# Seven half-width products in place of two full ones: a Strassen step over token halves in the first layer of one token group

## The chip, the cores and the metric

One core of a Trainium2 chip runs the kernel. The metric is device time in microseconds (us) of one launch; the kernel before takes 520.27 us, the median of 3 runs (520.02 to 520.69). The engines are named as in the profile: PE is TensorE (matmuls), PEld its weight loads, DVE is VectorE, ACT is ScalarE, POOL is GpSimd, SP is the engine on whose queue nearly all DMA transfers are issued.

## The reference

A linear attention with decay makes x, and two multilayer products follow. Everything is float32.

```
attn_out = _attn_ref(q, k, v, lam)         # 2 batches, 8 heads, 768 positions, 64 wide
x = attn_out.transpose(0, 2, 1, 3).reshape(1536, 512)

h = x @ w_in                               # 512 x 2048
x = maximum(0.01 * h, h) @ w_out           # 2048 x 512

a, b = x @ w1, x @ w2                      # 512 x 1024 each
out = ((a * b) @ w3) @ w_out2              # 1024 x 1024, 1024 x 512
```

## The kernel before

The 1536 tokens are worked on in three groups of 512, g = 0, 1, 2. The hidden width of 2048 is cut into 16 slices of 128, f = 0 to 15. A float32 operand is held as two halves in the type that TensorE takes, a high part and the rest, and one product of float32 matrices is three matmuls per piece (`EXACT`: high x high, low x high, high x low). Tokens are the moving side, so h comes out transposed, 128 hidden units by 512 tokens, in one PSUM bank.

For one slice and one group the first layer is `unit_h` (line 757 on): 4 chunks of the model width x 3 = 12 matmuls of 128x512 by `full` (line 731) into a PSUM buffer `ps`. ACT then applies the leaky step in place and copies the high part out, VectorE subtracts to get the low part (`pair_ops`, line 740). The second layer is `unit_y` (line 806): 12 matmuls of 128x512 by `products` (line 738) into four accumulators `acc`.

In the first 90 us the attention chunks are made, with slices 0 to 3 between them. The other slices come in blocks of four, b = 4, 8, 12. In such a block the groups 1 and 2 are taken together: `unit_hpair` (matmuls on line 1434) does the first layer for a pair of slices by Strassen's seven products over two slices and two groups, and `unit_joint` (line 1604) the second layer. It uses three PSUM buffers, one for each chain of sums. Group 0 is done slice by slice with `unit_h` and `unit_y`. `h_sums` makes the sums and differences of w_in that the seven products need (tile `sx`). Then `unit_w` (line 1297), the product of w_out with w1 and w2, `unit_pair` (line 1013) and `unit_out` (line 1200) follow.

The order of the instructions of each engine is written out by a list planner, `in_order` (line 81): each operation has a rank, a cost in ns (`CHIP`, `MB` for transfers), what it comes after, and the buffers that it takes and uses; an operation is put on its engine's list when the planner's clock says that its inputs and buffers are there, in the order of rank. Each engine then runs its list in order, and semaphores hold an instruction until its inputs are there. Transfers of weights go through a ring of `raw` buffers and are converted on ACT, VectorE and POOL (`top`, `u`, `f`: lines 328, 334, 352). Lines 224 and 228 are the helpers that write the high part and the low part of a pair.

Of the kernel before, what the change touches and what calls it, by code (L numbers as in the profile page):

```python
# [7 lines left out]
F32 = mybir.dt.float32  # L8
F32R = mybir.dt.float32r
# [5 lines left out]
ALU = mybir.AluOpType  # L15
# [17 lines left out]
EXACT = ((0, 0), (1, 0), (0, 1))  # L33
XB = (10,40,45,50,50,60,85,105)
XL = (10,40,125,50,50,60,145,165)
# [7 lines left out]
class Buf:  # L43
# [6 lines left out]
    def free(self, now):  # L50
        return all(u.end is not None and u.end <= now for u in self.users)


class Op:
# [5 lines left out]

    def __init__(self, cost, fn, rank, after=(), takes=(), uses=(), behind=(), port=False, lag=None, hold=0):
# [3 lines left out]
        self.lag, self.hold = lag, hold  # L65
        for b in (*takes, *uses):
            b.users.append(self)


EARLY = [32, 103, 104]  # L70
LATENCY = {"q": 3600}
MB = 2560
CHIP = {
    ("act", 680): 662, ("act", 580): 520, ("act", 560): 490, ("act", 500): 490, ("act", 350): 305, ("dve", 640): 602,
    ("dve", 680): 602, ("dve", 660): 602, ("dve", 400): 335, ("dve", 1180): 1135, ("pool", 1250): 1255,
    ("pool", 640): 700,
}
SEEN = {"dve": 115, "act": 130, "pool": 80, "pe": 100}

# [76 lines left out]
def tile_kernel(ctx: ExitStack, tc, qkv, lamb, w_in, w_out, w1, w2, w3t, wo, out):  # L156
# [32 lines left out]
    }  # L189
    pools.update({r: const for r in TAGS})  # L190
    ops = []

# [104 lines left out]
    def convert(kind, i, rank):  # L297
# [42 lines left out]
        def whole(e):  # L340
# [20 lines left out]
        o0 = op(  # L361
            {"q": MB / 2}, load, EARLY[len(loads) - 1] if len(loads) <= len(EARLY) else rank, takes=[raw], behind=late
        )
# [376 lines left out]
    def pair_ops(src_op, ps, rank):  # L740
# [12 lines left out]
        return buf, [o1, o2]  # L753

    gp, accs, acc_op, last_h = {}, {}, {}, []

# [19 lines left out]
    def accumulate(tag, g, f, nf, rank, w_ops, bufs, job, pairs, evac):  # L776
# [14 lines left out]

        if first and g == NG - 1:
            for c in range(4):
                after.append(op({"pe": 680}, mm([c], False), rank, after, [acc[c]], bufs, behind=after[-1:]))
            acc_op[tag, g] = after[-1]
            return
        if f % nf < nf - 1:
# [581 lines left out]
    hm_home = {}  # L1379
    sums = {}  # L1380

    def h_sums(f, rank):
# [11 lines left out]
        out = []  # L1394
        for get, after, fb in ((g0, [o2, o4], b0), (g1, [o1, o3], b1)):
# [8 lines left out]
        sums[f] = out  # L1404

# [107 lines left out]
    def unit_joint(b, rank, ranks):  # L1513
# [31 lines left out]
        def half(name, which, rank, after=lambda u: []):  # L1545
            out = []
            for u in two:
                d, o = hidden[u]
                buf = Buf("lp" if last else "part")
                parts.append(buf)  # L1550
# [4 lines left out]
                ops_ = halves_of(  # L1555
                    part, lambda t=d[which]: t.tile, [o[which], *opened], [buf], [d[which]], rank,
                    lambda buf=buf: new(buf, [P, 2, T], F32R), ("dve",) if last else ("dve", "pool"),
                )
                out.append((part, ops_, buf))
# [10 lines left out]

        last, parts = b == NF1 - FB, []
        opened = last_op if last else []
        r = ranks["make"]
# [61 lines left out]

    joint_pe, last_op = [], []

# [87 lines left out]
    for k, (g, f) in enumerate(steps[:-2]):  # L1725
        unit_y(g, f, r(k))
        for n, d in CHUNKS.get(k, {}).items():
            attention(n, r(k) + d, n % CPG > 0)
            if n % CPG == CPG - 1:
                outputs(n, r(k) + d + 2)  # L1730
        if steps[k + 2] == (0, FB):
            x_differences(r(k) + 20)
        unit_h(*steps[k + 2], r(k) + 10, r(k + 2))
    PP = (0, 10, 30, 35, 50, 60, 70)
    h_sums(FB, r(len(steps)))
    rank = r(len(steps) - 2)
    for b in range(FB, NF1, FB):
        last = b + FB == NF1
        if b in PAIRED:
            XO = XL if last else XB  # L1740
            unit_y(0, b, rank)
            unit_hpair(b, rank + XO[0])
            unit_h(0, b + 2, rank + XO[1], rank + XO[1] + 20)
            unit_y(0, b + 1, rank + XO[2])
            unit_h(0, b + 3, rank + XO[3], rank + XO[3] + 20)
            if last:
                last_part.append(Buf("xy"))
                last_op.append(
                    op({"dve": 50}, lambda e: new(last_part[0], [P, 2, NCC, T], F32R), rank, [last_h[-1]], [last_part[0]])
                )  # L1750
# [16 lines left out]
        if b in PAIRED:  # L1767
            unit_joint(b, rank + 120, {"sums": rank + 100, "make": rank + 100, "p": [rank + 120 + k for k in ((0, 10, 20, 30, 40, 50, 60) if last else PP)]})
            if not last:
                unit_h(0, b + FB, rank + 140, rank + 230)  # L1770
                unit_h(0, b + FB + 1, rank + 160, rank + 240)
                h_sums(b + FB, rank + 210)
        else:
# [97 lines left out]
```

## Time and profile before

| | |
|---|---|
| median of 3 runs | 520.27 us |
| the profiled execution | 520.21 us |
| its span, first to last instruction | 518.3 us |
| PE busy | 510.6 us, 99% of the span |
| PEld / DVE / ACT / POOL busy | 422.9 / 385.7 / 328.8 / 142.4 us |
| moved by DMA | 54.03 MB, 104 GB/s in the mean |

Busy times are sums over the span, so an engine that is busy 74% of the span in the mean can still be busy all the time in one stretch. A run of instructions in the chain of waits has a start, a length and a count; length by count is the distance from one to the next. The mean length of one matmul as shown elsewhere is longer than that distance, since matmuls overlap.

### The profile page before, as it was taken

To read this page: it belongs to the slowest core of one execution; us is meant where nothing else is said; L and a number is where in the kernel's file an instruction comes from. 1 tells how busy PE (TensorE), PEld (TensorE's weight loads), DVE (VectorE), ACT (ScalarE), POOL (GpSimd) and SP (SyncE) were. 2 spreads that over 40 slices of the span, in tenths; PEclk is the share of its full clock that TensorE was granted. 3 is DMA by queue.
4 is the path that set the end of the run, shared out by engine and by line. 5 is a ranking of instruction groups with operands and counts; after the bars stand their busy time and mean duration, and the time that the engine had idled before them with its cause. 6 is when DMAs were issued, how large, how long until landed. Compare 5 with 4: busy or idle time off the path is not lost.

```text
span 518.3 us, 8618 instructions
## 1 busy us (share of the span) xinstructions
PE 510.6 (99%) x3320; PEld 422.9 (82%) x3320; DVE 385.7 (74%) x640; ACT 328.8 (63%) x627; POOL 142.4 (27%) x128
## 2 busy tenths in 40 slices
PE   8999999999999999999999899999999999999997
PEld 7788887888888888888888688888888888888886
DVE  6876475997588964889799999888347865656951
ACT  5895765776757667457876796886347444454820
POOL 4331021401152411832222223010112635553200
PEclk9999999999999999999999999999999999999999
DMA  8983750222210501017240474870001000000102
GB/s 310 410 339 118 250 205 3 83 81 82 69 56 17 185 2 40 1 56 269 99 145 1 164 242 138 290 261 2 0 1 59 22 1 0 1 1 2 40 21 101
DMA packets 16024, 54.03 MB, mean 104 GB/s; under 512 B 1904, under 2 KB 2416, under 8 KB 15984
## 3 DMA queue, kind: packets, MB, share of 16 engines
q1 hardware_dynamic: 15552, 53.22, 29.2%
q8 instruction: 26, 0.43, 0.4%
q10 hardware_dynamic: 432, 0.27, 0.2%
q14 instruction: 14, 0.11, 0.1%
HBM read 50.34 MB, written 3.15 MB: 103 GB/s over the span
## 4 chain that ended last, share of the span: by engine, by line
PE 87%; DVE 6%; DMA 4%; ACT 1%; issue 1%; SPq 0%; DVEq 0%
PE ps L731 21%; PE acc L738 15%; PE ps L1013 15%; PE ps L1434 10%; PE ps L1297 7%; PE acc L1604 7%; PE acc L1200 5%; PE ps L640 3%; PE ps L1200 2%; DMA raw<-in_w_in_dram 2%; DVE xy L228 2%; DVE yf L1620 2%; DMA yf<-in_qkv_dram 1%; PE ps L720 1%; DVE dd L869 1%
## 5 line engine op out<-in xcount | busy, mean ns | idle before, releaser
L328 ACT CAST top<-raw 128x512 f16<-128x512 bf16 x72 | 56.0, 783 | 18.3 <-DVE few_f L352 7.5
L738 PE MATMUL acc<-act,wp 128*128 128x512 f32 x252 | 61.5, 392 | 0.0
L738 PEld LDWEIGHTS acc<-act,wp 128*128 128x128 f32 x252 | 46.9, 188 | 9.9
L731 PE MATMUL ps<-xy,wp 128*128 128x512 f32 x192 | 44.8, 389 | 0.0
L731 PEld LDWEIGHTS ps<-xy,wp 128*128 128x128 f32 x192 | 36.0, 188 | 7.5
L731 PE MATMUL ps<-xy,wi 128*128 128x512 f32 x168 | 40.9, 393 | 0.9 <-ACT xy L556 0.8
L731 PEld LDWEIGHTS ps<-xy,wi 128*128 128x128 f32 x168 | 31.1, 188 | 8.5 <-ACT xy L556 1.2
L1297 PE MATMUL ps<-wi,wp 128*128 128x512 f32 x144 | 34.7, 392 | 1.4 <-POOL wp L228 0.7
L1013 PE MATMUL ps<-xy,wp 128*128 128x512 f32 x144 | 34.2, 391 | 0.0
L1013 PE MATMUL ps<-xy,raw 128*128 128x512 f32 x144 | 33.9, 389 | 0.0
L334 ACT ACTIVATE u<-raw 128x512 uint32<-128x512 uint32 x50 | 33.4, 669 | 0.0
L1297 PEld LDWEIGHTS ps<-wi,wp 128*128 128x128 f32 x144 | 26.9, 188 | 7.9 <-POOL wp L228 1.2
L228 DVE TENSOR_TENSOR act<-ps,act 128x512 fp32r<-128x512 f32 x32 | 21.9, 684 | 13.7 <-ACT act L746 13.5
L1013 PEld LDWEIGHTS ps<-xy,wp 128*128 128x128 f32 x144 | 26.9, 188 | 6.1 <-DVE w L1031 0.4
L1013 PEld LDWEIGHTS ps<-xy,raw 128*128 128x128 f32 x144 | 27.0, 188 | 5.6
L1620 DVE TENSOR_TENSOR yf<-acc,yf 128x512 f32<-128x512 f32 x28 | 18.8, 684 | 7.1 <-PE acc L1604 7.1
L731 PE MATMUL ps<-xy,few_wi 128*128 128x512 f32 x96 | 23.1, 389 | 0.0
L738 PE MATMUL acc<-wp,act 128*128 128x512 f32 x96 | 22.9, 389 | 0.0
L767 ACT ACTIVATE ps<-ps 128x512 f32<-128x512 f32 x24 | 14.1, 588 | 11.2 <-PE ps L731 11.0
L738 PEld LDWEIGHTS acc<-wp,act 128*128 128x128 f32 x96 | 18.0, 188 | 3.7
L731 PEld LDWEIGHTS ps<-xy,few_wi 128*128 128x128 f32 x96 | 18.0, 188 | 3.7
L352 DVE SCALAR_TENSOR_TENSOR f<-u,top 128x512 uint32<-128x512 uint32 x26 | 18.2, 704 | 3.7 <-ACT u L334 3.6
(318 smaller groups left out, 1254.7 us busy)
## 6 DMA issues: line engine op xcount, KB each, us to landing
raw<-in_w_in_dram SPq DMA_DIRECT2D x16, 512.0 KB, 4.3
raw<-in_w_out_dram SPq DMA_DIRECT2D x16, 512.0 KB, 4.0
raw<-in_w3t_dram SPq DMA_DIRECT2D x16, 512.0 KB, 4.3
raw<-in_w_dram SPq DMA_DIRECT2D x16, 512.0 KB, 5.1
yf<-in_qkv_dram SPq DMA_DIRECT2D x14, 512.0 KB, 7.0
inp<-in_qkv_dram SPq DMA_DIRECT2D x10, 512.0 KB, 9.1
raw<-in_wo_dram SPq DMA_DIRECT2D x8, 512.0 KB, 4.5
out_dram<-f SPq DMA_DIRECT2D x10, 256.0 KB, 2.0
```

Of the source, the lines that this page charges most:

```text
L228: engines[e].tensor_tensor(out=dst(), in0=src(), in1=hi_().bitcast(F32), op=ALU.subtract)
L328: nc.scalar.copy(dst, src)
L334: nc.scalar.activation(out=t, in_=mid, func=AF.Copy, bias=4096.0)
L352: nc.vector.scalar_tensor_tensor(out=get().bitcast(U32), in0=u.tile, scalar=13, in1=top.tile, op0=ALU.logical_shift_right, op1=ALU.bitwise_or,
L731: nc.tensor.matmul(o, w(a)[:, cc * P : (cc + 1) * P], x(b, cc), start=k == 0, stop=k == 3 * NCC - 1)
L738: nc.tensor.matmul(o, st(a), mv(b), start=first and k == 0, stop=last and k == 2)
L1013: nc.tensor.matmul(ps.tile, w(a, kk), mv(b, kk), start=fresh and kk == 0 and i == 0, stop=kk == NCC // 2 - 1 and i == 2, skip_group_check= ...
L1200: nc.tensor.matmul(o, wl(v, t, c), mv(v2)[:, cut], start=begun and t == 0 and i == 0, stop=t == n - 1 and i == 2, skip_group_check=True,)
L1297: nc.tensor.matmul(ps.tile, w(a)[:, k * P : (k + 1) * P], wo_part[j](b), start=j == 0 and n == 0, stop=j == NF2 - 1 and n == 2,)
L1434: nc.tensor.matmul(ps.tile, w(a, kk), mv(b, kk), start=fresh and kk == 0 and i == 0, stop=kk == NCC // 2 - 1 and i == 2, skip_group_check= ...
L1604: nc.tensor.matmul(ps.tile, st[left][k][0](a, c), mv[right][k][0](b_), start=fresh and k == 0 and i == 0, stop=k == 1 and i == 2, skip_gro ...
L1620: nc.vector.tensor_tensor(out=y(), in0=ps.tile, in1=y(), op=ALU.add)
```

## The change

For the pairs of slices (6,7), (8,9), (10,11), (12,13) and (14,15) group 0's `unit_h` is replaced by `unit_hself`. It takes two slices and the two halves of the group's 512 tokens, and makes seven products over half of the model width: 2 chunks x 3 = 6 matmuls of 128x256 each, 42 for a pair in place of 24 of 128x512. Two PSUM buffers of 128x512, `one` and `two`, hold the results, and their halves are token halves. Three copies on ACT (line 1506) and three adds on VectorE (line 1513), all 128x256, combine the products.

The moving side of the products is seven forms of x: three of its corners (b11, b21, b22) and four sums (t1 to t4), each split in a high and a low part. `x_forms` makes them once, at step 6 of the attention phase, and stores them in DRAM (line 1412, 14 transfers); each pair loads its seven forms again (line 1480, 512 KB each, 35 loads) into four slots of a buffer that was opened for the last block only, and is now opened earlier. Beside that the second layer of group 0 is put later by a rank of 43, and for two of four slices it is written as four pieces of three matmuls; the ranks of one product, two costs of the planner and the order of `h_sums` change.

```diff
-XB = (10,40,45,50,50,60,85,105)
+XB = (10,40,45,50,15,60,85,105)
...
+PIECES = (0, 1)
+YB0 = 43
+SELF = (165, 170, 230)
...
-MB = 2560
+MB = 2660
...
+    def x_forms(rank):
...
+            def store(e):
+                t = forms[name] = dram.tile([P, 2, T], F32, tag=f"form_{name}", name=f"form_{name}")
+                for v in range(2):
+                    nc.sync.dma_start(out=t[:, v, :].rearrange("p (k n) -> p k n", n=h), in_=src(v))
...
+    def unit_hself(f, rank, rank_next, order=(0, 0, 0, 0, 0, 0, 0), ahead=30):
...
+        one, two = Buf("ps"), Buf("ps")
+        one_left, one_right, two_left = (one, slice(0, h)), (one, slice(h, T)), (two, slice(0, h))
...
+            def load(e):
+                t = new(mv, None)
+                nc.sync.dma_start(out=t.bitcast(F32), in_=forms[right])
...
+                for kk in range(NCC // 2):
+                    for i, (a, b) in enumerate(EXACT):
+                        nc.tensor.matmul(
+                            ps.tile[:, cut], w(a, kk), mv.tile[:, b, kk * h : (kk + 1) * h],
...
+                {"act": 350}, lambda e: nc.scalar.copy(new(buf, [P, T])[:, :h], ps.tile[:, cut]), rank_next, [o], [buf], [ps]
...
+                lambda e: nc.vector.tensor_tensor(
+                    out=ps.tile[:, dst], in0=ps.tile[:, cut], in1=t.tile[:, :h], op=ALU.add
...
+        p1 = product(0, one_right, "a11", "b11", [])
+        t1, k1 = keep(one_right, p1)
+        p7 = product(1, two_left, "s3", "t3", [])
+        p2 = product(2, one_left, "a12", "b21", [p1])
+        p6 = product(3, one_right, "s2", "t2", [k1])
+        t2, k2 = keep(one_right, p6)
+        c11 = add(slice(0, h), one_left, t1, [p2, k1])
+        p5 = product(4, one_right, "s1", "t1", [k2])
+        t4, k4 = keep(one_right, p5)
+        c22 = add(slice(h, T), two_left, t4, [p7, k4])
+        p3 = product(5, one_right, "s4", "b22", [k4])
+        p4 = product(6, two_left, "a22", "t4", [c22])
+        c21 = add(slice(0, h), two_left, t2, [p4, k2])
+        rest(f, one, [p3, c11])
+        rest(f + 1, two, [c21, c22])
...
-            unit_y(0, b, rank)
+            unit_y(0, b, rank + YB0)
             unit_hpair(b, rank + XO[0])
-            unit_h(0, b + 2, rank + XO[1], rank + XO[1] + 20)
+            weight("in", b + 2, 0, rank + XO[1])
             unit_y(0, b + 1, rank + XO[2])
-            unit_h(0, b + 3, rank + XO[3], rank + XO[3] + 20)
...
+            unit_hself(b + 2, rank + XO[1], rank + XO[1] + 20)
```

The first place is PE's list around the first pair, slices 6 and 7, in block 4. Line 1434 (1607 after) is `unit_hpair`, 731 (738 after) is `unit_h`, 738 (745 after) is `unit_y`, 1489 is `unit_hself`. Before:

```order
L1434 MATMUL ps<-inp,sx 128x512 x6
L1434 MATMUL ps<-xy,wi 128x512 x6
L1434 MATMUL ps<-inp,sx 128x512 x6
L738 MATMUL acc<-act,wp 128x512 x12
L1434 MATMUL ps<-xy,sx 128x512 x6
L1434 MATMUL ps<-xy,wi 128x512 x6
L731 MATMUL ps<-xy,few_wi 128x512 x12
```

And after, from the same product of `unit_hpair`:

```order
L1607 MATMUL ps<-inp,sx 128x512 x6
L1489 MATMUL ps<-xy,few_wi 128x256 x6
L1607 MATMUL ps<-xy,sx 128x512 x6
L1607 MATMUL ps<-xy,wi 128x512 x6
L1489 MATMUL ps<-xy,sx 128x256 x6
L1489 MATMUL ps<-xy,few_wi 128x256 x6
L1489 MATMUL ps<-xy,sx 128x256 x6
L745 MATMUL acc<-act,wp 128x512 x3
L1489 MATMUL ps<-xy,sx 128x256 x6
L745 MATMUL acc<-act,wp 128x512 x9
L1489 MATMUL ps<-xy,sx 128x256 x6
L1489 MATMUL ps<-xy,few_wi 128x256 x6
```

The products 1, 7, 2, 6, 5, 3 and 4 stand in that order; product 1 is where `unit_y` stood, 7, 2 and 6 stand one behind the other, and `unit_y` is now cut in two around product 5.

The second place is PE's list around the last pair, slices 14 and 15, in block 12. Before:

```order
L1434 MATMUL ps<-inp,sx 128x512 x6
L731 MATMUL ps<-xy,late_wi 128x512 x12
L1434 MATMUL ps<-xy,sx 128x512 x6
L1434 MATMUL ps<-xy,few_wi 128x512 x6
L731 MATMUL ps<-xy,late_wi 128x512 x12
L1434 MATMUL ps<-xy,late_wi 128x512 x6
```

And after:

```order
L1607 MATMUL ps<-inp,sx 128x512 x6
L1489 MATMUL ps<-xy,late_wi 128x256 x6
L745 MATMUL acc<-act,wp 128x512 x12
L1607 MATMUL ps<-xy,sx 128x512 x6
L1607 MATMUL ps<-xy,few_wi 128x512 x6
L1489 MATMUL ps<-xy,sx 128x256 x6
L1489 MATMUL ps<-xy,late_wi 128x256 x6
L1489 MATMUL ps<-xy,sx 128x256 x6
L745 MATMUL acc<-act,wp 128x512 x6
L1489 MATMUL ps<-xy,sx 128x256 x6
L745 MATMUL acc<-act,wp 128x512 x6
L1489 MATMUL ps<-xy,sx 128x256 x6
```

One more `unit_y` of 12 matmuls has come ahead of `unit_hpair`'s next pair, and is cut in two halves around product 5; the products 3 and 4 follow it.

The third place is SP's list, the issue of transfers, from the last weights of the first two layers to `wo`. Line 322 (329 after) loads weights. Before:

```order
L322 DMA raw<-in_w_out_dram 128x2048
L322 DMA raw<-in_w_in_dram 128x2048
L322 DMA raw<-in_w_out_dram 128x2048
L322 DMA raw<-in_w_in_dram 128x2048
L322 DMA raw<-in_w_out_dram 128x2048 x2
L322 DMA raw<-in_wo_dram 128x2048 x8
```

And after, with the loads of the forms on line 1480:

```order
L329 DMA raw<-in_w_out_dram 128x2048
L1480 DMA xy<-form_t_1513 128x2x512
L1480 DMA xy<-form_b_725 128x2x512
L1480 DMA xy<-form_t_1439 128x2x512
L329 DMA raw<-in_wo_dram 128x2048 x6
L1480 DMA xy<-form_t_1397 128x2x512
L329 DMA raw<-in_wo_dram 128x2048
L1480 DMA xy<-form_b_764 128x2x512
L1480 DMA xy<-form_t_1539 128x2x512
L329 DMA raw<-in_wo_dram 128x2048
```

The loads of forms stand between those of the weights on the one queue, and the last three among the eight loads of `wo`.

## Rows read from the trace of the kernel before

**Rows 1.** The page: span, busy time of the engines, granted clock in tenths.

```profile
span 518.3 us, 8618 instructions
...
PE 510.6 (99%) x3320; PEld 422.9 (82%) x3320; DVE 385.7 (74%) x640; ACT 328.8 (63%) x627; POOL 142.4 (27%) x128
...
PEclk9999999999999999999999999999999999999999
```

**Rows 2.** The waits of PE: us in total, times, longest.

```profile
PE acc L1708 <- POOL old L244: 1.1, 1, 1.1
PE ps L731 <- ACT xy L556: 0.8, 1, 0.8
PE ps L1297 <- POOL wp L228: 0.7, 1, 0.7
...
PE ps L1297 <- DVE wp L228: 0.7, 1, 0.7
```

**Rows 3.** The chain of waits at three places: start us, us, what.

```profile
87.44 0.52 PE ps L731 x2
...
87.97 5.28 PE ps L731 x22
...
115.00 2.72 PE acc L738 x12
...
509.21 4.15 PE acc L1200 x24
513.36 1.45 PE ps L1200 x12
```

**Rows 4.** The timeline at the end: start us, us, engine line op out<-in xcount.

```profile
508.82 0.39 PE L1200 MATMUL ps<-xy,raw 128*128 128x512 f32 x1
...
509.25 0.69 DVE L1238 TENSOR_TENSOR f<-ps,yf 128x512 f32<-128x512 f32 x1 [2.03 <-PE ps L1200]
...
513.20 1.60 PE L1200 MATMUL ps<-wi,raw 128*128 128x256 f32 x12
```

**Rows 5.** The timeline at the end, a narrow copy and a narrow add.

```profile
512.48 0.37 ACT L1274 COPY wp<-acc 128x256 f32<-128x256 f32 x1 [8.08 <-DVE wp L1274]
...
514.84 0.42 DVE L1272 TENSOR_TENSOR wp<-ps,ta 128x256 f32<-128x256 f32 x1 [2.44 <-PE ps L1200]
```

**Rows 6.** Busy time by stretch: us, PE, PEld, DVE, ACT, POOL, clock, DMA share, GB/s.

```profile
60.00:93.00 33.00, 32.93 (x536) 26.80 (x536) 20.87 (x35) 22.62 (x51) 5.72 (x5) 1.00 0.29 102
93.00:110.00 17.00, 17.00 (x77) 14.08 (x76) 16.96 (x29) 12.39 (x24) 5.38 (x5) 1.00 0.34 118
...
250.00:270.00 20.00, 20.00 (x90) 16.52 (x89) 19.06 (x31) 16.55 (x32) 6.39 (x5) 1.00 0.45 157
270.00:290.00 20.00, 19.31 (x86) 15.65 (x84) 20.00 (x34) 12.47 (x22) 4.83 (x4) 1.00 0.09 27
```

**Rows 7.** The timeline of PE around the start of line 1297.

```profile
288.92 0.39 PE L1297 MATMUL ps<-wi,wp 128*128 128x512 f32 x1
290.04 4.17 PE L1297 MATMUL ps<-wi,wp 128*128 128x512 f32 x17 [0.73 <-POOL wp L228]
...
295.40 0.49 PE L1297 MATMUL ps<-wi,wp 128*128 128x512 f32 x1
296.58 0.73 PE L1297 MATMUL ps<-wi,wp 128*128 128x512 f32 x2 [0.69 <-DVE wp L228]
```

**Rows 8.** Transfers: KB each, median us from issue to landing.

```profile
raw<-in_w_out_dram SPq DMA_DIRECT2D x16, 512.0 KB, 4.0
...
raw<-in_w_dram SPq DMA_DIRECT2D x16, 512.0 KB, 5.1
...
raw<-in_wo_dram SPq DMA_DIRECT2D x8, 512.0 KB, 4.5
```

More of the change, by code (lines that the diff above doesn't have):

```diff
@@ L50, in free, with __init__ @@
     def free(self, now):
-        return all(u.end is not None and u.end <= now for u in self.users)
+        return all(u.end is not None and (u.seen if u.slow else u.end) <= now for u in self.users)
 class Op:
-    def __init__(self, cost, fn, rank, after=(), takes=(), uses=(), behind=(), port=False, lag=None, hold=0):
+    def __init__(self, cost, fn, rank, after=(), takes=(), uses=(), behind=(), port=False, lag=None, hold=0, slow=False):
         self.cost, self.fn, self.rank, self.takes, self.behind, self.port = cost, fn, rank, takes, behind, port
@@ L70 @@
 EARLY = [32, 103, 104]
+PIECES = (0, 1)
+YB0 = 43
+SELF = (165, 170, 230)
+FORMS = 6
+FORM_RANK = 5
 LATENCY = {"q": 3600}
-MB = 2560
+MB = 2660
 CHIP = {
@@ L77 @@
 }
+PAUSE = 1200
 SEEN = {"dve": 115, "act": 130, "pool": 80, "pe": 100}
@@ L361, in convert @@
         o0 = op(
-            {"q": MB / 2}, load, EARLY[len(loads) - 1] if len(loads) <= len(EARLY) else rank, takes=[raw], behind=late
+            {"q": MB / 2 + (PAUSE if len(loads) == 1 else 0)}, load, EARLY[len(loads) - 1] if len(loads) <= len(EARLY) else rank, takes=[raw], behind=late
         )
@@ L753, in pair_ops @@
         return buf, [o1, o2]
+    pieces = {}
     gp, accs, acc_op, last_h = {}, {}, {}, []
@@ L790, in mm @@
             return fn
-        if first and g == NG - 1:
+        if first and g == NG - 1 or tag == "y" and f in PAIRED and f % nf in PIECES:
             for c in range(4):
-                after.append(op({"pe": 680}, mm([c], False), rank, after, [acc[c]], bufs, behind=after[-1:]))
+                after.append(
+                    op(
+                        {"pe": 680}, mm([c], False), rank, after, [acc[c]] if first else [],
+                        [*([] if first else [acc[c]]), *bufs], behind=after[-1:],
+                    )
+                )
             acc_op[tag, g] = after[-1]
+            if g == 0 and f % nf == 1:
+                pieces.setdefault(f // 4 * 4 + 2, []).extend(after[-4:])
             return
@@ L1382, in h_sums, with open_parts @@
+    parts = []
+    def open_parts(rank):
+        last_part.append(Buf("xy"))
+        opened.append(
+            op({"dve": 50}, lambda e: new(last_part[0], [P, 2, NCC, T], F32R), rank, [last_h[-1]], [last_part[0]])
+        )
+    opened = []
     def h_sums(f, rank):
@@ L1394, in h_sums @@
         out = []
-        for get, after, fb in ((g0, [o2, o4], b0), (g1, [o1, o3], b1)):
+        for get, after, fb in ((g1, [o1, o3], b1), (g0, [o2, o4], b0)):
             buf = Buf("sx" if f in PAIRED or f == NF1 - FB else "sq")
@@ L1403, in h_sums @@
             out.append((buf, o))
-        sums[f] = out
+        sums[f] = out[::-1]
     def unit_hpair(f, rank):
@@ L1549, in half @@
                 buf = Buf("lp" if last else "part")
-                parts.append(buf)
+                if last:
+                    parts.append(buf)
                 def part(v, buf=buf):
@@ L1555, in half @@
                 ops_ = halves_of(
-                    part, lambda t=d[which]: t.tile, [o[which], *opened], [buf], [d[which]], rank,
+                    part, lambda t=d[which]: t.tile, [o[which], *(opened if last else [])], [buf], [d[which]], rank,
                     lambda buf=buf: new(buf, [P, 2, T], F32R), ("dve",) if last else ("dve", "pool"),
@@ L1569, in change @@
                 )
-        last, parts = b == NF1 - FB, []
-        opened = last_op if last else []
+        last = b == NF1 - FB
         r = ranks["make"]
@@ L1730, in tile_kernel @@
                 outputs(n, r(k) + d + 2)
+        if k == FORMS:
+            x_forms(r(k) + FORM_RANK)
         if steps[k + 2] == (0, FB):
@@ L1769, in tile_kernel @@
             if not last:
-                unit_h(0, b + FB, rank + 140, rank + 230)
-                unit_h(0, b + FB + 1, rank + 160, rank + 240)
-                h_sums(b + FB, rank + 210)
+                weight("in", b + FB, 0, rank + 140)
+                weight("in", b + FB + 1, 0, rank + 160)
+                h_sums(b + FB, rank + SELF[0])
+                unit_hself(b + FB, rank + SELF[1], rank + SELF[2])
         else:
```

106 lines of the change are left out of this document (99 added, 7 removed).

## The prediction

> **What bounds the kernel now.** I read the first part of the page first, then TensorE's waits, then the chain of waits, then stretches. The reader is to see one engine that hardly ever stops. TensorE (PE) is busy 510.6 of a span of 518.3 us, at a granted clock that stays at the 2.4 GHz level; VectorE (DVE) is next with 385.7 [rows 1]. The view of PE's waits holds little: 1.1 us early, 0.8 us near the start, and two waits of 0.7 us for VectorE and GpSimd (POOL) at line 1297 [rows 2]. So a matmul taken away is worth its whole pitch, and a wait put between two matmuls costs its whole length.
>
> The pitch comes from the chain: 12 matmuls of 128x512 take 2.72 us, 226.7 ns each; at the end of the program 12 of 128x256 take 1.45 us, 121 ns, and a mixed run of 12 + 12 takes 4.15 us, which leaves 1.43 us, 119 ns, for the narrow ones [rows 3]. I take 120 ns. Half the columns cost 53%, not half.
>
> **Columns.** Each of group 0's five pairs of slices had 24 matmuls of 128x512: 24 x 226.7 = 5.44 us. Now it has 7 products of 6 matmuls of 128x256: 42 x 120 = 5.04 us. That is 0.40 us a pair (0.33 at 121.6, 0.45 at 119), **-2.0 us** for five, bounds -1.7 and -2.2.
>
> A rule bears on this, in sentences by themselves. The Trainium skill, "TensorE: Matmul & The Clock Gate", section "Wait — 56ns, not 53.3ns?", gives a warm start-to-start of N / 2.4 GHz + 2.5 ns, so 216 and 109 ns; by it the columns would give 24 x 216 - 42 x 109, 0.6 us a pair, 3.0 us in all. The trace's 226.7 and 120 are each 11 ns longer, and 42 instructions pay that more often than 24, so the measurement decides for -2.0.
>
> **Waits that the change adds.** In the seven products each PSUM buffer is filled by halves, and three results must leave the right half of the first buffer (by copies on ScalarE, ACT, line 1506) before the next product may be written there; three adds on VectorE (line 1513) follow. In the built program the semaphores order the two halves of a buffer as one: the first copy, k1, waits for product 2 where that stands before it, and not for product 1 alone; the add c11 waits for what was last written in the buffer, and the second copy k2 for c11. The price of one hand-over: a narrow matmul ends 1.60 - 11 x 0.12 = 0.28 us after its start; the next engine starts 0.04 us later (PE's last wide result begins at 508.82, lasts 0.39, VectorE begins at 509.25) [rows 4]; a narrow copy on ACT takes 0.37, a narrow add on VectorE 0.42 [rows 5]; 0.05 back to PE, an estimate from the 0.04. With PE's own pitch of 0.12 taken off, product -> copy -> product costs 0.28 + 0.04 + 0.37 + 0.05 - 0.12 = 0.62 us, product -> copy -> add -> product 0.62 + 0.46 = 1.08, and so does product -> add -> copy -> product. What PE has in between is taken off:
> - Pair (6,7): product 2 is followed at once by product 6, which waits for k1: 0.62. Product 6 is followed by three wide matmuls (0.68) and product 5, which waits through c11 and k2: 1.08 - 0.68 = 0.40. The nine that follow (2.04) cover the rest.
> - Pair (10,11): the same order, but product 6 waits for c11 too: 1.08. Then 0 to 0.1.
> - Pair (14,15): 0.62 to 0.99 at product 6, since ACT first writes other narrow halves; six wide matmuls (1.36) cover the next.
> - Pairs (8,9) and (12,13): six to twelve wide matmuls (1.36 to 2.72) stand between the products: nothing.
> - The groups-1-and-2 product p3 of slices 4, 5 has lost the 12 matmuls ahead of it and now has six narrow ones (0.72): 0.39 + 0.04 + a wide copy, at most VectorE's 0.69 + 0.05 - 0.23 = 0.94, so at most 0.22, taken as 0.1.
>
> Sum: 0.62 + 0.40 + 1.08 + 0.05 + 0.70 + 0.10 = **+2.95 us**. Bounds: 2.3 if the hand-overs shown contain slack, 4.5 if ACT or VectorE is in the middle of a wide instruction (0.69 [rows 4]) at two of the places.
>
> The rule that speaks against this layout is told by itself: the Trainium skill, "PSUM — Partial Sum Buffer", section "PSUM bank collisions raise a hardware error", asks to guard PSUM by bank and quadrant, not by address, since disjoint columns of one bank collide too. By it these waits can't be shortened while both halves lie in one bank; that the halves could be used side by side would make the term about 1 us. No row of the trace before shows two halves in use, the waits in the program agree with the rule.
>
> **A wait that goes.** From 87.44 us 24 matmuls take 0.52 + 5.28 = 5.80 us where 24 pitches are 5.44 [rows 3]: 0.36 is lost, most of it, I take it, to the late last chunk of x. Now nine matmuls of the other product stand in between: **-0.25 us** (0 to -0.36).
>
> **The last stage before line 1297.** From 270 to 290 us VectorE is busy 20.00 of 20 us, from 250 to 270 19.06 [rows 6]: here VectorE, not PE, sets the end, and PE pays at line 1297, once from 288.92 to 290.04 (0.89 over the pitch) and once from 295.40 to 296.58 (0.95) [rows 7]. What VectorE has to do there changes in two ways: three narrow adds of the last pair come in, which I count at 3 x 0.42 = 1.26, and one multiplication by w_out of group 0 is made earlier, so about two wide instructions at 20.00 / 34 = 0.59 us [rows 6] leave the stretch: -1.2. The balance is 0; bounds -1.8 (both waits gone) and +0.8. What hides the columns of the last pair is the same: PE's saving there turns into waiting.
>
> **The forms.** Forming t1 to t4 and their halves adds 14 wide additions and subtractions and 4 copies. They fall between 60 and 110 us. VectorE is busy 20.87 of 33 us from 60 to 93 and POOL 5.72, but 16.96 of 17 from 93 to 110 [rows 6]; the sums of weights that lie there now come later. Room of 12 us on VectorE alone against 14 x 0.59 = 8.3: taken as 0, up to +1.5 if the last two forms miss the first pair.
>
> **Loads.** 14 stores of 256 KB and 35 loads of 512 KB come onto SP's queue. A load of that size lands in 4.0 us (w_out), 4.5 us (wo) at the median [rows 8]. Each form has one of four slots; the last two forms of a pair can be loaded only when two products before them have freed theirs, and PE has 4.7 to 5.3 us of other work in between. Taken as 0; if a landing takes 0.5 us more than that room in each pair, +2.5.
>
> **Sum** against the profiled execution (518.3 of span + 1.9 around it = 520.21): -2.0 + 2.95 - 0.25 + 0 + 0 = +0.7, so **520.9 us**. That execution lies 0.06 us below the median of the runs shown, 520.27; no correction is made. What a measurement can tell from no change is 0.2%, 1.04 us: same is 519.2 to 521.3. The forecast's own range is 520.2 to 521.6.
>
> **Rivals.**
> - *The last stage keeps the gain.* VectorE's work after the last pair gets shorter, and both waits at line 1297 go: 520.9 - 1.8 = 519.1; with hand-overs at their lower bound 518.5. For it: the multiplication moved forward; the waits are late by under 1 us each. Against it: 20.00 of 20 us busy, with three adds more. Chance 0.25.
> - *Forms land late* (slower). Place: product 3 and product 4 of each pair, and above all of (14,15), where eight loads of wo stand on the same queue. Price: 0.4 to 0.5 us a pair, 520.9 + 2.0 = 522.9. It decides as soon as a form takes more than about 5 us from its slot's release; the median of loads of w already is 5.1 in a stretch where several run together [rows 8]. Against it: DMA is idle most of the time here. Chance 0.17.
> - *In-order engines behind the copies.* k1, k2 and k4 stand in ACT's order among wide copies, the adds in VectorE's full stretch: two or three hand-overs pay another 0.3 to 0.7 us: 521.9. Chance 0.18.
> - *The skill's pitch*, by the rule above: 3.0 for 2.0 and 519.9; what rows make of it is the bound of 119 ns, 520.7, inside the forecast. Chance 0.02.
>
> The forecast holds 0.38. Faster by over 0.2% takes the first rival but for its upper edge: 0.22; slower takes the second, most of the third and the upper edge of the forecast: 0.35; 0.43 stays within. The range goes from 518.6, the first rival's middle, to 522.8.
>
> **What would show it.** Right: 210 matmuls of 128x256 at 120 ns; PE waits for ACT's copy at product 6 of pairs (6,7) and (14,15) of 0.5 us each by the waits view, for VectorE at (10,11) of about 1, none in (8,9) and (12,13); waits at line 1297 of 1 to 2 us in sum. Wrong: waits of PE for DMA at product 3 or 4; idle PE before the first pair; or no wait of PE for copies at all, in which case the halves run side by side and the time comes out near 518.

## The result, and the profile after

The changed kernel takes 525.39 us, the median of 5 runs (522.83 to 526.09), against 520.32 us for the kernel before (5 runs, 520.02 to 521.04): a ratio of 1.0086, with a 95% interval of 1.0059 to 1.0113. The forecast was 520.9, with a range from 518.6 to 522.8. The runs of the changed kernel spread over 3 us, those of before over 1 us.

The profiled execution took 524.58 us. Its page, the lines that answer to [rows 1]:

```profile
span 522.8 us, 8995 instructions
...
PE 512.5 (98%) x3410; PEld 426.7 (82%) x3410; DVE 395.9 (76%) x651; ACT 337.0 (64%) x652; POOL 163.6 (31%) x146
...
PEclk9999999999999999999999899999999999999999
```

TensorE has less to do and is busy longer, and one slice of the clock shows an 8. The waits of TensorE, against [rows 2]:

```profile
PE ps L1489 <- DVE ps L1513: 1.7, 2, 1.0
PE ps L1489 <- ACT ta L1506: 1.3, 3, 0.5
PE acc L1881 <- POOL old L251: 1.1, 1, 1.1
PE ps L1312 <- POOL wp L235: 0.9, 1, 0.9
PE ps L454 <- DMA yf<-in_qkv_dram: 0.9, 1, 0.9
PE ps L1312 <- ACT wp L231: 0.8, 1, 0.8
PE ps L1607 <- ACT ta L1619: 0.3, 1, 0.3
PE ps L1777 <- DVE xy L235: 0.2, 1, 0.2
```

Line 1489 is the new product. Five waits stand there: three for ACT's copy, two for VectorE's add, and none for a transfer. A sixth stands beside them: the product of groups 1 and 2 next to (6,7), on line 1607. Where the five lie, in the timeline of TensorE (start us, us, what; the idle time before it in brackets), in the pairs (6,7), (10,11) and (14,15):

```profile
127.16 0.88 PE L1489 MATMUL ps<-xy,sx 128*128 128x256 f32 x6
127.87 0.88 PE L1489 MATMUL ps<-xy,few_wi 128*128 128x256 f32 x6
129.27 0.98 PE L1489 MATMUL ps<-xy,sx 128*128 128x256 f32 x6 [0.52 <-ACT ta L1506]
130.09 0.86 PE L745 MATMUL acc<-act,wp 128*128 128x512 f32 x3
131.24 0.98 PE L1489 MATMUL ps<-xy,sx 128*128 128x256 f32 x6 [0.30 <-ACT ta L1506]
132.06 2.23 PE L745 MATMUL acc<-act,wp 128*128 128x512 f32 x9
...
188.79 0.88 PE L1489 MATMUL ps<-xy,few_wi 128*128 128x256 f32 x6
190.65 0.98 PE L1489 MATMUL ps<-xy,sx 128*128 128x256 f32 x6 [0.98 <-DVE ps L1513]
...
249.44 0.88 PE L1489 MATMUL ps<-xy,late_wi 128*128 128x256 f32 x6
250.84 0.98 PE L1489 MATMUL ps<-xy,sx 128*128 128x256 f32 x6 [0.52 <-ACT ta L1506]
...
255.15 0.87 PE L1489 MATMUL ps<-xy,sx 128*128 128x256 f32 x6
256.73 0.98 PE L1489 MATMUL ps<-xy,late_wi 128*128 128x256 f32 x6 [0.71 <-DVE ps L1513]
...
282.31 1.88 PE L1777 MATMUL ps<-xy,wp 128*128 128x512 f32 x7 [0.22 <-DVE xy L235]
```

The last line lies in the joint stage (`unit_joint`, line 1777), which `unit_w` on line 1312 follows.

The price of a wait is read from start to start. Six narrow matmuls from 127.16 to 127.87 are 0.71 us; from 127.87 to 129.27 it is 1.40, so 0.68 is lost, where the bracket says 0.52: the bracket leaves out the time in which the last matmul is still shown running. And the six that follow last 0.82 to the next run, not 0.72. Each wait costs its bracket, 0.16 and another 0.1.

Where the time went between the two profiled executions, by the starts of the same products:
| stretch | us |
|---|---|
| to the first product of groups 1 and 2 (120.28 before, of which 2.72 for 12 matmuls that now come later; 116.21 after) | -1.4 |
| columns: 5 x 24 wide against 5 x 42 narrow | -2.0 |
| six waits in and beside the pairs, with their slow restarts | +4.9 |
| joint stage, up to line 1312: waits of 0.5 and 1.0 | +1.5 |
| other pauses in that stretch, each under 0.4, which no row puts down to one cause | +1.2 |
| line 1312: one wait of 1.2 in place of two of 2.1 in sum, a lower clock +1.6 | +0.7 |
| the end of the program after the last matmul | -0.5 |
| sum (522.8 - 518.3) | +4.4 to 4.5 |

### The profile page after: what moved, and what is told of

Same layout as the page of the kernel before. It is cut to its first block, busy times and chain, and to the rows that moved or that the text cites. A ratio compares the mean times of both kernels' runs of the same rounds, so it can differ in the third digit from the quotient of the medians.

```text
span 522.8 us, 8995 instructions
## 1 busy us (share of the span) xinstructions
PE 512.5 (98%) x3410; PEld 426.7 (82%) x3410; DVE 395.9 (76%) x651; ACT 337.0 (64%) x652; POOL 163.6 (31%) x146
## 4 chain that ended last, share of the span: by engine, by line
PE 86%; DVE 6%; ACT 4%; DMA 2%; issue 1%; POOL 0%; SPq 0%; ACTq 0%; DVEq 0%; POOLq 0%
PE ps L738 15%; PE ps L1028 15%; PE acc L745 14%; PE ps L1312 9%; PE ps L1607 9%; PE acc L1777 7%; PE acc L1215 5%; PE ps L1489 4%; PE ps L647 3%; PE ps L1215 2%; PE acc L454 2%; DMA raw<-in_w_in_dram 1%; DVE xy L235 1%; DVE yf L1793 1%; DMA yf<-in_qkv_dram 1%
## 5 line engine op out<-in xcount | busy, mean ns | idle before, releaser
L738 PE MATMUL ps<-xy,wp 128*128 128x512 f32 x192 | 44.8, 389 | 0.0
L738 PE MATMUL ps<-xy,wi 128*128 128x512 f32 x168 | 40.6, 393 | 0.0
L1312 PE MATMUL ps<-wi,wp 128*128 128x512 f32 x144 | 36.0, 404 | 1.7 <-POOL wp L235 0.9
L1312 PEld LDWEIGHTS ps<-wi,wp 128*128 128x128 f32 x144 | 28.1, 196 | 8.4 <-ACT wp L231 1.3
L341 ACT ACTIVATE u<-raw 128x512 uint32<-128x512 uint32 x48 | 32.1, 668 | 0.0
L359 DVE SCALAR_TENSOR_TENSOR f<-u,top 128x512 uint32<-128x512 uint32 x26 | 19.3, 751 | 3.2 <-ACT u L341 2.9
L1489 PEld LDWEIGHTS ps<-xy,sx 128*128 128x128 f32 x120 | 16.6, 189 | 4.8 <-ACT ta L1506 2.4
L1489 PE MATMUL ps<-xy,sx 128*128 128x256 f32 x120 | 18.0, 286 | 2.3 <-ACT ta L1506 1.3
L235 POOL TENSOR_TENSOR wp<-inp,wp 128x512 fp32r<-128x512 f32 (+1 forms) x6 | 7.2, 1202 | 41.4 <-ACT wp L231 41.4
```

The costliest lines, as they stand in the source:

```text
L235: engines[e].tensor_tensor(out=dst(), in0=src(), in1=hi_().bitcast(F32), op=ALU.subtract)
L341: nc.scalar.activation(out=t, in_=mid, func=AF.Copy, bias=4096.0)
L738: nc.tensor.matmul(o, w(a)[:, cc * P : (cc + 1) * P], x(b, cc), start=k == 0, stop=k == 3 * NCC - 1)
L1312: nc.tensor.matmul(ps.tile, w(a)[:, k * P : (k + 1) * P], wo_part[j](b), start=j == 0 and n == 0, stop=j == NF2 - 1 and n == 2,)
L1489: nc.tensor.matmul(ps.tile[:, cut], w(a, kk), mv.tile[:, b, kk * h : (kk + 1) * h], start=fresh and kk == 0 and i == 0, stop=kk == NCC // ...
```

## The experiments

All ratios are to the kernel before on the same chip. Three theories ran through them: W, waits of TensorE at the hand-overs plus a later last stage; F or L, the forms' forming and transfers; I, late instructions. Other letters stand for a rival in one run, told where that run's expectation is.

**e0, the changed kernel again.** 

> The changed kernel once more, unedited. Theory W: 522.8 to 526.1 again, the same waits at the same products within 0.2 us in every execution, and the spread comes from the last stage and from whether the granted clock falls to its lower level behind the two waits at line 1312. Rival F: the waits move from run to run, with landings of transfers.

523.90 us (522.48 to 524.89), 1.0075 [1.0062, 1.0088]. In its profiled execution (522.48) the same waits stand at the same products: 0.68, 0.47, 1.15, 0.68 and 0.87 from start to start, within 0.01 of the first one; the sixth, beside (6,7), is 0.37 for 0.50. The clock stayed up in all five runs, and they still spread by 2.4 us, so the clock isn't what makes this spread. Two executions of one program, the windows behind line 1312 (us, busy time of PE, PEld, DVE, ACT, POOL, then the granted clock), first the changed kernel:

```profile
293.00:295.30 2.30, 1.24 (x4) 0.85 (x5) 1.71 (x4) 2.30 (x5) 1.28 (x1) 1.00 0.19 45
295.40:298.70 3.30, 3.30 (x9) 2.56 (x8) 3.30 (x7) 1.61 (x4) 0.00 (x0) 0.50 0.78 267
298.80:305.00 6.20, 6.20 (x29) 5.11 (x28) 5.77 (x11) 5.47 (x10) 0.00 (x0) 1.00 0.57 184
```

then the same again:

```profile
294.90:298.20 3.30, 3.30 (x16) 2.75 (x15) 3.30 (x7) 1.63 (x4) 0.00 (x0) 1.00 0.80 259
```

In 3.3 us 9 matmuls went through at 1.2 GHz and 16 at 2.4: 7 x 0.227 = 1.6 us. What TensorE did before is the same in both, two waits of 0.85 us, 1.4 us apart:

```profile
293.19 0.49 PE L1312 MATMUL ps<-wi,wp 128*128 128x512 f32 x1 [0.85 <-ACT wp L231]
294.55 1.82 PE L1312 MATMUL ps<-wi,wp 128*128 128x512 f32 x5 [0.86 <-POOL wp L235]
```

So the fall is a matter of the execution; in the first five runs three had the lower mean clock (0.997) and two not. Seven traces of this page have the same two waits (0.80 to 0.86 us by the bracket): in four of them (the changed kernel, e2, e3, e4) the clock falls behind the second one, in three (e0, e8, e11) it does not.

**e1, no pairs.**
```diff
+AT = ()
...
-        if k == FORMS:
+        if k == FORMS and AT:
...
-            unit_hself(b + 2, rank + XO[1], rank + XO[1] + 20)
+            if own:
+                unit_hself(b + 2, rank + XO[1], rank + XO[1] + 20)
```
Where a pair isn't in `AT` (`own` is false), `unit_h` is called as before, and the sums of the weights are made at their old place.

> The changed kernel with all five pairs of group 0 made by the old 24 wide matmuls; no forms are made, stored or loaded. What stays are the other edits (second layer of group 0 later and in pieces, planner costs). Theory W (the loss is waits of TensorE at the hand-overs inside the pairs, plus a later last stage): the 5.0 us of waits and the 2.0 us of saved columns both go; the attention phase keeps the 1.36 us that it gained, the last stage is as before: 519.0 us. Rival F (forming, storing and loading the forms is what costs): also back to 520.3 or less, but with the attention phase then shorter by more than 1.36 us against the changed kernel. If the later second layer is what harms the last stage: 521 or more.

519.70 us over 12 runs, 0.9997 [0.9985, 1.0009], in two groups: seven runs of 518.85 to 519.72 with a mean clock of 0.999 or 1.0, five of 520.83 to 521.54 with 0.996 or 0.997. Theory W gave 519.0 and meets the first group. Where the clock stays up, the other edits thus bring about 1.1 us. They bring a risk too: the two waits on the line of `unit_w` have come together, here 1.2 us apart. The trace is of a run of the first group; where in the runs of the second one the clock fell, no trace shows.

```profile
294.64 0.50 PE L1313 MATMUL ps<-wi,wp 128*128 128x512 f32 x1 [0.92 <-ACT wp L232]
295.80 2.56 PE L1313 MATMUL ps<-wi,wp 128*128 128x512 f32 x10 [0.65 <-DVE wp L236]
```

Before they lie 6.5 us apart [rows 7], and no run of that kernel had a mean clock under 0.998. Pairs and forms went together in e1, so it doesn't tell W from F; e2 and e4 bear on that.

**e2, pairs (12,13) and (14,15) only.**
```diff
+AT = (12, 14)
```


> The changed kernel with the Strassen step for slices (12,13) and (14,15) only; the other three pairs as before; the forms are still made and stored, 14 loads instead of 35. Theory W: columns -0.8, waits of (14,15) +1.75, none in (12,13), last stage +2.1, attention phase -1.36: 522.0 us. Rival F (forming and transfers): most of the +5 stays, 524 or more.

523.18 us (521.57 to 525.21), 1.0059 [1.0041, 1.0077]. By the median it is between W's 522.0 and F's 524; the profiled execution took 521.84. The trace has the two waits of (14,15), 0.68 and 0.86 from start to start, none in (12,13), and those of 0.38 and 1.0 in the joint stage (line 1778 here) and at its end:

```profile
PE ps L1313 <- ACT wp L232: 0.8, 1, 0.8
PE ps L1490 <- DVE ps L1514: 0.7, 1, 0.7
...
PE ps L1490 <- ACT ta L1507: 0.5, 1, 0.5
PE ps L1778 <- DVE xy L236: 0.2, 1, 0.2
```

e6, e9 and e10 below keep the other pairs and make this one wide, and have none of these four: the last pair brings them. The median is left between: two runs with the clock up took 521.57 and 523.07, so the spread is there with two pairs as with five.

**e3, the second layer spread over the pairs.**
```diff
-        p2 = product(2, one_left, "a12", "b21", [p1])
-        p6 = product(3, one_right, "s2", "t2", [k1])
+        p2 = product(2, one_left, "a12", "b21", [p1, k1])
+        c11 = add(slice(0, h), one_left, t1, [p2, k1])
+        p6 = product(3, one_right, "s2", "t2", [k1, c11])
...
-        for o in pieces.pop(f, []):
-            o.behind = [*o.behind, p6]
+        ys = pieces.pop(f, [])
+        if ys:
+            for o, before, then in ((ys[0], p7, p2), (ys[1], p2, p6), (ys[2], p6, p5), (ys[3], p5, p3)):
+                o.behind = [*o.behind, before]
+                then.behind = [*then.behind, o]
```


> All five pairs, but in pairs (6,7), (10,11) and (14,15) the four pieces of the second layer (3 wide matmuls each) are put one behind each of the products 7, 2, 6 and 5, and product 2 is ordered after the first copy, product 6 after the add c11. Same matmuls. Theory W: each hand-over has 0.68 us of other matmuls; the 4.3 us of waits in these three pairs fall to about 1, the last stage stays: 521.5 us. Rival Q (ACT and VectorE are late for reasons of their own, so the place of the fillers doesn't matter): waits of 3 us or more stay, 524 or more.

523.93 us (522.30 to 528.53), 1.0081 [1.0052, 1.0110]. W was right on the waits and wrong on the time. The profiled execution is the slowest of the six, 528.53:

```profile
PE ps L1489 <- DMA xy<-form_t: 2.4, 2, 1.8
PE ps L647 <- issue: 2.2, 1, 2.2
...
PE ps L1489 <- ACT ta L1506: 0.4, 1, 0.4
```

The waits for copies and adds have shrunk from 3.0 to 0.4, and two other kinds have come. The form t4 lands late at product 4 of (6,7), and at (14,15): the rival "forms land late" of the prediction, in its place. The granted clock falls to 1.2 GHz twice in this execution: at 139 us, behind the wait of 1.8 us for the form, and at 299.5 us, behind the two waits before and on line 1312. These two are the same as in the changed kernel, and so is the 0.38 in the joint stage. And TensorE stops for 2.2 us in the attention phase with nothing that released it ("issue"). The chain there, and the DMA queues of 38 to 43 us and 43 to 48 us (packets, MB, share):

```profile
45.00 0.75 PE ps L647 x48
45.75 2.25 issue
48.00 0.85 PE ps L647 x27
```

```profile
q1 hardware_dynamic: 779, 1.39, 96.1%
...
q1 hardware_dynamic: 701, 1.05, 60.3%
...
q8 instruction: 1, 0.02, 1.2%
```

In the run e0 the first of these windows, 38 to 43 us, looks otherwise:

```profile
q1 hardware_dynamic: 810, 1.50, 96.5%
q8 instruction: 1, 0.02, 1.2%
```

A transfer of instructions that e0 has at 40.4 us comes at 45.6 us in e3, and TensorE stops from 45.75 to 48.00. From 38 to 45.5 us the DMA engines are full, 94% to 98% in e0 as in e3, with the stores of b11, b21 and b22 among the rest; in the stop itself they are busy for 21%. e4 had the same stop (1.5 us), e11 too (2.3 us), with that transfer at 44.8 and 45.8 us. In the other traces of kernels that make forms it comes between 38.4 and 40.6 us, and there is no such stop. Of the four kernels that make no forms (before, e1, e12, e13) no trace had the stop either. That the late transfer causes it is likely, and not shown.

**e4, half of each load.**
```diff
-                nc.sync.dma_start(out=t.bitcast(F32), in_=forms[right])
+                if turn["lp"] < RINGS["lp"]:
+                    nc.sync.dma_start(out=t.bitcast(F32), in_=forms[right])
+                else:
+                    nc.sync.dma_start(out=t[:, 0, :].bitcast(F32), in_=forms[right][:, 0, :])
```


> The changed kernel, but after the first four loads of forms each load brings the high half only (256 KB in place of 512); the low halves used are those left in the slot, so group 0's products of the pairs are not exact. Instructions and order on all engines but the transfers are the same. Theory L (part of the loss, and the spread of 2 to 3 us from run to run, is forms that land late; the rest is the waits at the hand-overs): the fastest runs stay at 522.5 us, the median comes down from 524 to 525 to about 522.7. Rival N (transfers are hidden, the spread has another cause): median 524 to 525, spread as before.

524.90 us (522.75 to 527.51), 1.0079 [1.0051, 1.0107]. The halved loads land in 2.8 us (b) and 3.1 us (t) at the median (3.8 and 4.9 in the changed kernel), and nothing is won: rival N. The loads are not what makes the changed kernel slow, as long as the waits give them time.

**e5, each load twice.**
```diff
                 nc.sync.dma_start(out=t.bitcast(F32), in_=forms[right])
+                nc.sync.dma_start(out=t.bitcast(F32), in_=forms[right])
```


> The changed kernel with each form loaded twice into the same slot (35 more transfers of 512 KB). Theory L: a form has 4.7 to 5.3 us from its slot's release to its use and takes 4.9 at the median, so a second load adds 2 to 4 us at product 3 or 4 of each pair: 530 us or more, with TensorE waiting for DMA there. Rival N: a cover of more than one load's time, at most 526.

616.82 us, 1.1848. It doesn't measure what it was to: the second load into the slot waited for the first, and with it SP's whole queue.

```profile
SPq L1481 <- DMA xy<-form_t: 88.4, 20, 6.5
...
SPq L1481 <- DMA xy<-form_b: 63.9, 15, 5.3
```

It says only that a wait at the head of that queue holds the weights behind it back. The mean granted clock was 0.925 to 0.931 in its runs, and TensorE was busy for 536.1 us in place of 512.5, so not all of the 92 us is waiting.

**e6, the last pair wide.** (14,15) takes 24 wide matmuls, on x stored in DRAM and loaded in 4 pieces.
```diff
-            unit_hself(b + 2, rank + XO[1], rank + XO[1] + 20)
+            (unit_hwide if b + 2 in WIDE_AT else unit_hself)(b + 2, rank + XO[1], rank + XO[1] + 20)
```


> The Strassen step for pairs (6,7) to (12,13); (14,15) by the old 24 wide matmuls, their x loaded from DRAM into the same four slots (4 loads in place of 7; 8 more stores once). Theory W: against the changed kernel's undisturbed 522.5 us, 1.75 us of waits inside the last pair and 1.5 us of waits at the end of the joint stage go, 0.4 us of columns come back: 519.7 us; waits at line 1312 again as in the kernel before, 0.9 us each and some 1.5 us or more apart. Rival S (the last stage is late for other reasons, as the later second layer): only the 1.75 goes, 521.2.

523.98 us, 1.0065 [1.0050, 1.0081], not 519.7. From the first product of groups 1 and 2 to the line of `unit_w` it took 173.67 us against 176.53 in e0: -2.86, where W said -2.85. The waits of the last pair and of the joint stage are gone; those left moved a little, so that the two numbers are this close is luck: at (6,7) there is one wait of 1.14 from start to start for 0.68 and 0.47, and beside it 0.64 for 0.37. But the attention phase, into which its eight more stores came, ended 3.2 us later, with waits there of 1.8 and 0.6 us for x. The stage was right, the kernel around it was not held.

**e7, only (8,9) and (12,13).**
```diff
-WIDE_AT = (14,)
+WIDE_AT = (6, 10, 14)
```


> The Strassen step for pairs (8,9) and (12,13) only, the two that showed no wait; (6,7), (10,11), (14,15) by wide matmuls on x loaded from DRAM. Theory W: no waits inside pairs, columns -0.8 us, attention phase -1.1: 518.3 us where the granted clock stays up, 520.3 where it falls behind line 1312. Rival L2 (loads land late even for wide matmuls): waits of TensorE for DMA of 1 us or more, 520 or more everywhere.

525.88 us, 1.0111 [1.0086, 1.0137]. It has the same late attention phase, new waits in the joint products (1.0, 0.6 and 0.4 us for ACT's and VectorE's parts), and one of 1.0 us inside (8,9), a pair that had shown none. W's 518.3 is off by 7.6; the order written for one set of pairs doesn't carry over to another.

**e8, the stores of b11, b21, b22 later.**
```diff
+        calm = [*ready, x_done[2 * CPG]]
...
-                ready, [xs[0]],
+                calm, [xs[0]],
```


> The changed kernel; the six stores of b11, b21 and b22 wait until chunk 8 of x is made (some 20 to 30 us later), after the stretch in which the DMA engines are full. Nothing else is edited. Theory I (TensorE's instructions come late behind the stores in that stretch: a stop of 1.5 to 2.2 us at line 647 without a releaser in some executions): the first product of groups 1 and 2 starts by 116.3 us in the profiled execution, the runs with the clock up lie at 522.3 to 523.0, median 522.8. Rival (spread has another source): median 524 to 525, spread of 2 us among the runs with the clock up.

523.85 us, 1.0073 [1.0056, 1.0089]. The first product of groups 1 and 2 starts at 116.28, as theory I said, but the four runs with the clock up are 522.75 to 524.07: they still spread by 1.3 us, and the median lies between the two expectations. There is no stop in its trace, as there was none in the two of the changed kernel, so this run doesn't decide on theory I. Its trace shows in part where the time went: product 4 of (14,15) now waits for its form, among the loads of `wo`.

```profile
257.90 0.95 PE L1490 MATMUL ps<-xy,late_wi 128*128 128x256 f32 x6 [1.47 <-DMA xy<-form_t]
```

**e9 and e10, all of it mended, with and without the spreading.** e8's stores, e6's last pair, and in e9 also e3's order.

> Late stores, the four pieces of the second layer spread over the pairs (6,7) and (10,11), and (14,15) by wide matmuls on x loaded from DRAM. Theory W with I: attention phase -1.4, columns -1.6, waits inside the pairs +0.8, last stage as in the kernel before: 518.2 us, where no form lands late. Rival L (with the waits gone the forms of products 3 and 4 are the next to be late, 0.8 to 2 us a pair in pairs (6,7) and (10,11)): 520 to 521.

> As the run before, without the spreading: the pairs (6,7) and (10,11) keep the order of the changed kernel. Theory W: +2.2 us against the spread one (waits of 2.0 to 2.1 in (6,7) with its neighbour and 1.25 in (10,11)), 520.2 us. Rival L: the waits give the forms time, so it is no slower than the spread one.

e9: 521.91 us (521.28 to 522.22), 1.0031 [1.0019, 1.0042]; e10: 522.40 us, 1.0054 [1.0038, 1.0069]. The spreading is worth 0.5 us of the 2.2 expected, and the intervals touch; in the traces the stretch from the first product of groups 1 and 2 to the line of `unit_w` takes 172.92 us in e9 and 173.37 in e10. Both wait for a late split of x before 88 us, 2.0 us in e9 and 1.5 in e10; without it e9 would be near 519.9 by this estimate, which no run tests. The waits view of e9 has 0.4 us at the new products and 0.4 at those of groups 1 and 2, and no form is late: rival L is not borne out here.

**e11, short adds in the last pair.**
```diff
+            n = 16 if f == 14 and dst == cut else h
```


> The changed kernel; in the pair (14,15) the two adds that work in place (c11 and c21) take 16 columns in place of 256, so its first slice is not whole. Same instructions, order and waits. Theory D (the adds' own time on the full VectorE makes the last stage late): about 0.5 us less work there, the wait of 1.0 us before line 1312 and that of 0.4 us in the joint products fall together by about 0.5 us. Rival O (the order does it: what VectorE does in that stretch, and the late start of it behind the waits of the pair): they stay within 0.1 us, and the wait of 0.87 us at product 4 stays, since VectorE is in a longer instruction when its add becomes ready.

525.08 us, 1.0095 [1.0079, 1.0111]. The waits of 0.38, 0.96 and 1.13 (start to start) at the end of the joint stage are within 0.05 of the changed kernel's: rival O. So it isn't the adds' own time, and by e3, where the copies and adds of that pair were no longer waited for and these waits stayed, it isn't the pair's waits for them either. That the order of the work in that stretch makes it late is what is left; no run changed that order alone. The wait at product 4 fell to 0.62 from 0.86, where rival O had let it stay.

**e12, the kernel before with two of the planner's costs.**
```diff
-MB = 2560
+MB = 2660
+PAUSE = 1200
```
`PAUSE` is added to the planner's cost of the first load of weights.

> The kernel before with two of the planner's costs of the changed one (MB 2660, and the first load longer by PAUSE); no other edit. Theory C (these move the attention chunks and give the 1.1 to 1.4 us that the attention phase gained): the first product of groups 1 and 2 about 1 us earlier, time 519.1 us, spread as before. Rival Y (the gain comes with the later second layer): 520.2.

519.81 us over 11 runs, 0.9989 [0.9980, 0.9998]. The first product of groups 1 and 2 starts at 119.38 for 120.28: the wait of 0.8 us for x at the start [rows 2] is gone. Theory C is right on the 0.9 us at that place; of the 1.1 us that it gave for the whole, the median shows 0.4.

**e13, no pairs, the second layer as before.**
```diff
-YB0 = 43
-PIECES = (0, 1)
+YB0 = 0
+PIECES = ()
```


> As the run without pairs, and the second layer in one piece and at its old rank. Theory K (the clock falls where the waits for the first two weights at line 1312 lie within 1.3 us of each other, as they do with the later second layer): waits apart again as in the kernel before (6 us), no run with the clock down, 519.1 us in all. Rival: the two groups of runs, 519.0 and 521.2, stay.

519.56 us over 11 runs (519.33 to 519.74), 0.9983 [0.9974, 0.9992]. Theory K is met on the clock: no run has a mean clock under 0.999. The waits aren't apart again as in the kernel before; there is one in place of two. Theory K's bound of 1.3 us isn't borne out elsewhere: in four traces the clock fell behind waits 1.4 us apart, and in the traces of e6, e9 and e10, with waits 1.1 us apart on that line, it stayed up.

```profile
288.84 0.51 PE L1313 MATMUL ps<-wi,wp 128*128 128x512 f32 x1
290.50 4.16 PE L1313 MATMUL ps<-wi,wp 128*128 128x512 f32 x17 [1.15 <-POOL wp L236]
```

It has the lowest median here, 0.7 us under the kernel before, and no Strassen step for group 0. What it keeps of the change are the planner's numbers around that step, so these are what helps.

## Why the prediction was wrong

- **Columns**: right. 210 matmuls at 120 ns, -2.0.
- **Waits inside the pairs**: the mechanism and most places were right, the term was too small: +2.95 forecast, +4.9 measured, above the upper bound of 4.5. This is the term that failed most. (6,7): 0.62 and 0.40 forecast, 0.68 and 0.47 measured. (10,11): 1.08 and 1.14. (14,15), product 6: 0.70 and 0.68. What was left out: the slow restart, 0.1 after each of six waits; 0.5 in place of 0.1 at the product of groups 1 and 2 next to (6,7), since ACT writes other results first; and 0.86 at product 4 of (14,15), which was taken as covered. The rival "in-order engines behind the copies" had named this mechanism for the last two, with 521.9. At product 4 VectorE is in a wide instruction of 1.80 us when c22 becomes ready; the bound for "in the middle of a wide instruction" had been 0.69.

```profile
254.41 1.38 POOL L235 TENSOR_TENSOR wi<-few_f,wi 128x512 fp32r<-128x512 f32 x1 [3.63 <-ACT wi L231]
...
254.53 1.80 DVE L884 TENSOR_TENSOR dd<-dd 128x512 f32<-128x512 f32 x1
...
256.25 0.42 DVE L1513 TENSOR_TENSOR ps<-ps,ta 128x256 f32<-128x256 f32 x1
```

  The instruction is that long beside work on POOL. Of the fourteen of its kind in this trace eight run beside none and take 0.68 to 0.69 us; the four over 1 us all run beside a POOL instruction, and two beside one are not longer. At 0.69 us it would have ended at 255.22 and c22 at 255.64, before product 4's turn at 255.87: by this estimate, which no run tests, the wait at product 4 would be gone.

  The Trainium skill, "PSUM — Partial Sum Buffer", section "PSUM bank collisions raise a hardware error", says to guard by bank and quadrant, not by address. The trace agrees with what the prediction drew from it: no copy of a right half ran beside a product into the left one. The program's semaphores forbade it, so no run here shows what would happen if one did.
- **Other pauses**: +1.2, the sum of many short ones between the same two places, which no term of the sum held.
- **The last stage**, taken as 0 from a balance of VectorE's work: this step failed on the place, and on the clock. The waits before line 1312 cost 1.5 us more, and those on it 0.9 less: +0.6, inside the bound of +0.8. What went beyond it are 1.6 us of lower clock, in some executions. e2 with e6, e9 and e10 puts the waits on the last pair, e11 shows that it isn't the adds' time. The balance counted work, not when each result comes. That the wait before the first weight at line 1312 would sit 1.4 us before the next, and the clock follow, was on no list of rivals.
- **The wait that goes**: too small. -0.25 forecast, -1.4 measured. The 24 matmuls that took 5.80 us [rows 3] take 5.44 in the changed kernel, so the 0.36 went whole; the wait of 0.8 us for x near 23 us went as well, through two planner costs that the prediction had not priced (e12).
- **Loads**: 0 in the two traces of the changed kernel, as forecast. The rival holds in e3 and e8, at the places that it named; it came when the waits that hid it went, or when the stores moved.
- **The range** rested on one time per kernel. The execution of e0 that was profiled, 522.48 us, lies inside it, the median of 525.39 outside. Three things differ from run to run: the clock behind line 1312 (1.6 us, seen in two executions of the changed kernel, down in one and up in the other), the stop without a releaser in the attention phase (1.5 to 2.3 us), and late forms (0.8 to 2.0 us). The last two were seen in variants of it, not in its own two traces, the faster ones of their series; how much each adds to the changed kernel's median of 525.39 is left open, as is what delays the instructions.

## What to carry to other kernels

A saving of 0.4 us per pair can't pay for one exposed hand-over between engines of 0.6 to 1.1 us: count the hand-overs of a cheaper algorithm before its columns, and add to each the drain of the last matmul and the slow restart. Where an engine is full, a balance of its work doesn't say when each result comes; look for what is queued ahead of the one that is waited for, and for what runs beside it on another engine. Two short waits of TensorE close together can cost more than two far apart: here the clock fell behind them in some executions, and a kernel that was steady got two times.

## What the runs showed of the hardware that was not expected

- The granted clock fell to the 1.2 GHz level in one execution and not in another of the same program, behind two waits of 0.85 us, 1.4 us apart; of seven traces with these waits four show it. In e1, whose trace has waits of 0.92 and 0.65 us, 1.2 us apart, 5 of 12 runs had the lower mean clock and were 2.0 us slower. Behind waits 6.5 us apart, or a single one of 1.15 us, no trace showed it. Behind a single one of 1.8 us the trace of e3 did, behind single ones of 1.5 to 2.0 us those of e6, e7, e9 and e10 did not.
- The first matmul after a wait keeps the next one off by 0.1 us more than the pitch, for 128x512 and 128x256 alike; behind the three waits for a transfer in e3 and e8 it is 0.07.
- One kind of VectorE instruction, 0.68 to 0.69 us in eight of fourteen places, took 1.0 to 1.8 us in four where an instruction on POOL ran beside it.
- TensorE stopped for 1.5 to 2.3 us with no semaphore to blame in three traces, and in these a transfer of instructions came at 44.8 to 45.8 us, which in the other kernels with forms came at 38.4 to 40.6. The DMA engines were full before it (94% to 99% from 38 to 43 us), but so they were in e0, without a stop (98%). That one causes the other is not shown.
- A second load into a slot held SP's queue until the first had landed: with 35 more loads the kernel took 92 us more, some of it at a lower clock.
